# Attention, top-1 mixture of experts and gated MLP on one core: paced scatters of token numbers, five gating groups, and the last four tiles' rows on GpSimd's queue

## The chip, the core and the metric

One core of a Trainium2 chip runs the whole program. The metric is device time of one execution in microseconds (us). Before the change the median of three runs is 1510.78 us (1508.44 to 1511.18). The engines are TensorE (PE; PEld is its weight load), VectorE (DVE), ScalarE (ACT), GpSimd (POOL) and SyncE (SP), which here only issues DMAs.

## The reference, cut to what matters

```python
k_p, v_p = mean over groups of 8 tokens of k, v        # 576 -> 72 keys per head
attn = softmax(q @ k_p.T / sqrt(64)); x = attn @ v_p   # (8, 8, 576, 64)
x = x.transpose(0, 2, 1, 3).reshape(4608, 512)

logits = x @ w_gate; e_idx = argmax(logits)            # 8 experts, one per token
gate_w = softmax(logits)[e_idx]; eom = sigmoid(x @ w_output_gate)
out[token] = gate_w * eom[e_idx] * (relu(x @ w1[e_idx]) @ w2[e_idx])

h = out @ w_in; return (h * sigmoid(h)) @ w_out        # 512 -> 2048 -> 512
```

## The kernel before

The program has three stages: attention with the gating (to about 217 us of the profiled execution), the expert products (to about 700 us), and the gated MLP. All order is written out by hand: an engine runs its instructions in the order in which the Python code emits them, and so does each DMA queue.

**Attention.** The 4608 tokens are 36 tiles of 128 (`NT`). A tile is two steps `u` (four heads each), so the main loop runs `u` from 2 to 74. A step turns the probabilities of one half tile on TensorE (`turn_p`, line 485), copies them on ScalarE (`copy_p`, line 489: this copy occurs once in each step, and the text counts steps by it), takes maxima on VectorE (line 473), exponentials on ScalarE (line 479), multiplies by the values (line 500) and makes the scores of a later step (line 463). At even steps `rows_out` divides a tile's sums on VectorE into `xg` (line 520) and stores the tile's 128 rows of 2 KB to DRAM, `xd` (line 527): tiles 0 to 31 from SP's queue, tiles 32 to 35 from ScalarE's (`ACT_AT = 32`). A table, `plan`, filled by `at(u, f)`, says what else a step starts: loads of q in packets of 128 bytes (line 340), loads of k and v, their sums over 8 tokens on GpSimd (`pool_kv`, lines 358 to 364), zeroing of value tiles (`start_v`, lines 375 and 376). A second list, `item`, holds the transposes of the pooled keys and values (`tr_k` line 394, `tr_v` line 413, `rows_v` line 426), one for each step from its due step on.

**Gating.** Tiles are taken in groups, `GROUPS = (16, 8, 6, 6)`. When the last tile of a group has its gate values, the 20 operations of `gate_ops` (lines 551 to 618) go on the list `bgq`, from which each step takes two to four (`bg`): maximum, winning expert, rank of each token among those of its expert (`rank`, on TensorE, lines 566 and 569), slot number `sli`, and weight, which lands in `idw` beside the token's number. Then `scatter(i)` (lines 580 and 581) writes the 128 pairs (token number, weight) of one tile, 8 bytes each, into `idd`, a table in DRAM sorted by expert, with an indirect DMA of GpSimd's queue whose row numbers are `sli`. Ahead of each stands one memset of a single element, `spacer`. `SCAT` says at which step each scatter is emitted; as GpSimd's stream goes on without waiting for steps, a scatter starts when what stands ahead of it on GpSimd is done and its group's `idw` is there. Those of the last group and those due after the loop come in the next stage's head (`pre[-2]`, `pre[-0.5]`).

**Early item.** After the first 24 tiles (`EARLY = 2` groups) the expert with the most tokens is known: `early_ops` finds it, an indirect DMA fetches 384 of its token numbers (`e_gid`, line 638, at step `EG`), and at step `ET` they are copied and turned to `e_ids`. With these, GpSimd gathers the first item's rows from `xd` (line 1104, `gather_x`), so that the expert stage can start (transposes at line 1126, first product at line 1156) before the last group is gated.

Of the kernel before, what the change touches and what calls it, by code (L numbers as in the profile page):

```python
# [25 lines left out]
POOL = 8  # L26
NK = S // POOL
NT = N // P
GROUPS = (16, 8, 6, 6)
NG = len(GROUPS)  # L30
N9 = NK // 8
SB = B // 2
KPARTS = ((0, 4), (4, 8), (8, 9))
G0 = [sum(GROUPS[:g]) for g in range(NG)]
NBLK = N // P
# [2 lines left out]
KINDS = (3, 2, 1)  # L38
NKD = len(KINDS)
SLOTS = ((NBLK - 3 + E - 1) // 3, 2 * E, E)  # L40
EARLY = 2
REST = N - 3 * P
TB = 384
PREP = 112
# [18 lines left out]
QPB = 5  # L63
QA = 3
PVL = 3
ACT_AT = 32
EG = 63
ET = 70

SCAT = ((11, 3), (5, 3), (6, 2))  # L70
LOADS = (
# [44 lines left out]
def kernel(  # L116
# [14 lines left out]
    nc = tc.nc  # L131
# [55 lines left out]
    spacer = const.tile([1, 1], F32, tag="spacer", name="spacer")  # L187
# [134 lines left out]
    sums, vbt, qz_t, rank_t, bgq, evac, items_q, scq = {}, {}, {}, [], [], [], [], []  # L322
# [59 lines left out]
    def flush():  # L382
        while evac:
            evac.pop(0)()
# [123 lines left out]
    def o4(t):  # L508
        return pv_t[t].rearrange("p a (h c) -> p a h c", c=VW)
# [8 lines left out]
    def rows_out(t):  # L518
        xg = gx.tile([P, DM], F32, tag="xg", name=f"xg{t}")
        nc.vector.tensor_tensor(  # L520
            out=xg.rearrange("p (a h d) -> p a h d", a=2, h=4),
            in0=o4(t)[:, :, :, 0:D],
            in1=r_t[t].to_broadcast([P, 2, 4, D]),
            op=ALU.mult,
        )
        eng = nc.scalar if t >= ACT_AT else nc.sync
        return lambda: eng.dma_start(out=xd[t * P : (t + 1) * P, 0:DM], in_=xg)

    def gates(t):
        g = max(j for j in range(NG) if G0[j] <= t)  # L530
        if t == G0[g]:
            gl_t[g] = (lp if g == NG - 1 else gp).tile([P, GROUPS[g], 16], F32, tag="gl", name=f"gl{g}")
        gh = gp.tile([P, 2, 4, 16], F32, tag="gh", name=f"gh{t}")
# [7 lines left out]
    def gate_ops(g, pool, rank_ps):  # L541
        gl = gl_t.pop(g)
        GT = GROUPS[g]
        sh = [P, GT, E]
# [32 lines left out]

        def scatter(i):
            t = G0[g] + i
            nc.gpsimd.memset(spacer, 0.0)  # L580
            ins = nc.gpsimd.indirect_dma_start(
                out=idd,
                out_offset=bass.IndirectOffsetOnAxis(ap=sli[:, i, :], axis=0),
                in_=idw[:, t, :],
                in_offset=None,
            )
            tc.declare_no_dep(ins.ins, group="scat", reason="every token has a slot of its own")
            tc.add_to_no_dep_group("scat", ins.ins)
# [5 lines left out]
        ops = [  # L594
            red(mx, lg, ALU.max),
            tt(cand, lg, bc(mx), ALU.is_equal),
            tt(cand, cand, bc(wrev.unsqueeze(1)), ALU.mult),
            red(best, cand, ALU.max),
            tt(ohb, cand, bc(best), ALU.is_equal),
            rank,  # L600
            tt(oh, cand, bc(best), ALU.is_equal),
            tt(ex[:, :, 0:E], lg, bc(mx), ALU.subtract),
# [141 lines left out]
    def at(u, f, *a):  # L744
        plan.setdefault(u, []).append((f, a))
# [18 lines left out]
    def bg(n):  # L764
        while n and bgq:
            f = bgq[0]
            if f is None:
                bgq.pop(0)
                return
            bgq.pop(0)()  # L770
            n -= 1
# [6 lines left out]
    UN = 2 * NT  # L778
    for u in range(2, UN + PVL):
        for f, a in plan.get(u, ()):  # L780
            f(*a)
        flush()
        if u < UN:
            turn_p(u)
        if u + 2 < UN:
            maxima(u + 2)
        if u < UN:
            copy_p(u)
        if u + 2 < UN:
            exps(u + 2)  # L790
        if u >= PVL:
            values(u - PVL)
        if u + 3 < UN:
            scores(u + 3)
        if item and item[0][0] <= u and not rank_t:
            _, f, *a = item.pop(0)
            f(*a)
        t, odd = divmod(u - PVL - 2, 2)
        if odd == 0 and 0 <= t < NT:
            inverse(t)  # L800
            at(u + 2, rows_out(t))
        if odd and 0 <= t < NT:
            gates(t)
            if t + 1 in G0:
                g = G0.index(t + 1) - 1
                ops, scat = gate_ops(g, gp if g < NG - 2 else lp, rank_ps)
                bgq.extend(ops)
                for i, f in enumerate(scat):
                    v = u + SCAT[g][0] + 2 * i // SCAT[g][1]
                    if v < UN + PVL:  # L810
                        at(v, f)
                    else:
                        kept_scat.append(f)
                if g + 1 == EARLY:
                    ops, ga, tu, tv = early_ops()
                    bgq.extend(ops)
                    at(EG, ga)
                    at(ET, tu)
                    item.append((ET, tv))
        if u % 2 == 0 and QD <= u // 2 + QA < NT:  # L820
            emit_qT(u // 2 + QA)
        bg(2 if u < 52 else 4 if u < 58 or u >= 64 else 3)
    assert not item, item
    bg(len(bgq) + 1)
    flush()
# [537 lines left out]
    with ExitStack() as cctx:  # L1363
# [184 lines left out]
        for n in range(NFP, NFP * NSB):  # L1548
            k11, k21, k22, k12 = (n, 0, 0), (n, 1, 0), (n, 1, 1), (n, 0, 1)
            u, v, t = ctile("u", f"u{n}"), ctile("v", f"v{n}"), ctile("t", f"t{n}")  # L1550
# [72 lines left out]
```

## Time and profile before

| what | value |
|---|---|
| median of three runs | 1510.78 us |
| the profiled execution's own time | 1503.53 us |
| its span, first to last instruction | 1501.8 us |
| busy: PE, PEld | 1438.1 us (96%), 1274.9 us (85%) |
| busy: DVE, ACT, POOL | 935.1, 652.1, 380.4 us |
| mean granted TensorE clock | 0.976 of full speed |

The profiled execution took 1.7 us more than its span, and 7.25 us less than the median of the runs. TensorE is the engine that sets the pace of the whole program, but a busy TensorE is not one at full speed: its clock is granted at one of two levels, 2.4 GHz (1.00 in the profile) and 1.2 GHz (0.50), and its busy time counts both alike. So the first thing to look for is where its clock is below 1.00, and the second what stood still just before.

### The profile page before, as it was taken

The numbers are of one execution on the slowest core, as the hardware profiler recorded it, in microseconds if no ns is written. First come the engines' busy times: TensorE is split into PE (matmuls) and PEld (weight loads), VectorE is DVE, ScalarE is ACT, GpSimd is POOL, SyncE is SP. The second block draws the span as 40 slices with busy tenths as digits, with TensorE's granted clock in tenths as the row PEclk, the third lists the DMA queues.
The fourth block names the chain that finished last, engine by engine and source line by source line (L and its number), as shares of the span: only waits on it lengthen the run. The fifth ranks groups of instructions, "written<-read, shape, count | busy, mean of one in ns | idle before, by whom it ended". The sixth has DMA issues, their size and how long they took to land.

```text
span 1501.8 us, 21992 instructions
## 1 busy us (share of the span) xinstructions
PE 1438.1 (96%) x7924; PEld 1274.9 (85%) x7924; DVE 935.1 (62%) x1691; ACT 652.1 (43%) x1311; POOL 380.4 (25%) x445
## 2 busy tenths in 40 slices
PE   8998978899999999999999999999999999999996
PEld 6897867789889989898888898888888888898885
DVE  6675556698888778884762645555554555465443
ACT  4765343465665554663332423432343243234222
POOL 1766222345445534431011200030030012001001
PEclk9998688999999999999999999999999999999998
DMA  9999145687788876874989565476457647645441
GB/s 261 274 249 150 36 132 165 218 271 239 265 288 285 298 226 224 296 232 134 309 298 255 212 174 169 161 197 174 156 175 167 183 154 197 178 139 190 160 134 43
DMA packets 259624, 302.87 MB, mean 202 GB/s; under 512 B 157848, under 2 KB 190619, under 8 KB 250674
## 3 DMA queue, kind: packets, MB, share of 16 engines
q1 hardware_dynamic: 247042, 271.06, 61.7%
q0 software_dynamic: 11456, 28.48, 5.2%
q10 hardware_dynamic: 1008, 1.84, 0.4%
q8 instruction: 64, 1.05, 0.3%
q14 instruction: 54, 0.44, 0.1%
HBM read 251.70 MB, written 50.41 MB: 201 GB/s over the span
## 4 chain that ended last, share of the span: by engine, by line
PE 43%; DVE 4%; ACT 3%; issue 1%; SPq 0%; DMA 0%; POOL 0%; another core or an unknown queue 0%; DVEq 0%; ACTq 0%; POOLq 0%
PE o L1437 23%; PE b L1393 9%; PE a L1393 6%; DVE sg L1411 1%; ACT gh L1414 1%; DVE gl L1419 1%; ACT ems L1509 1%; DVE W L1499 1%; SPq L969 0%; DMA yin<-yd 0%; ACT os L1447 0%; ACT b L993 0%; DVE ems L1510 0%; DVE b L994 0%; POOL out_dram L1449 0%
## 5 line engine op out<-in xcount | busy, mean ns | idle before, releaser
L1437 PE MATMUL o<-woh,gh 128*128 128x512 f32 x576 | 229.2, 398 | 2.9 <-ACT gh L1414 2.4
L1437 PE MATMUL o<-woh,gl 128*128 128x512 f32 x576 | 229.5, 398 | 0.0
L1437 PE MATMUL o<-wol,gh 128*128 128x512 f32 x576 | 225.5, 391 | 0.0
L1449 POOL DMA_INDIRECT out_dram<-os,ids x33 | 35.7, 1082 | 623.3 <-ACT os L1447 619.4
L1414 ACT CAST gh<-sg 128x384 fp32r<-128x384 f32 x192 | 98.6, 513 | 148.7 <-DVE sg L1411 145.4
L1419 DVE TENSOR_TENSOR gl<-sg,gh 128x384 fp32r<-128x384 f32 x192 | 107.3, 559 | 75.5 <-ACT gh L1414 64.6
L1437 PEld LDWEIGHTS o<-woh,gl 128*128 128x128 f32 x576 | 107.9, 187 | 29.7 <-DVE gl L1419 3.5
L1437 PEld LDWEIGHTS o<-woh,gh 128*128 128x128 f32 x576 | 108.0, 188 | 22.2 <-ACT gh L1414 6.4
L1437 PEld LDWEIGHTS o<-wol,gh 128*128 128x128 f32 x576 | 108.2, 188 | 18.1
L1393 PE MATMUL a<-b,wA 128*128 128x384 f32 x480 | 97.4, 339 | 2.3 <-issue 1.8
L1393 PE MATMUL b<-t,wS 128*128 128x384 f32 x480 | 97.2, 337 | 0.2
L1407 ACT ACTIVATE sg<-a 128x384 f32<-128x384 f32 x56 | 27.5, 490 | 160.9 <-PE a L1393 160.9
L1393 PEld LDWEIGHTS a<-b,wA 128*128 128x128 f32 x480 | 85.2, 188 | 7.0 <-issue 2.7
L500 PE MATMUL pv<-vb,pT 72*128 72x128 f32 (+1 forms) x640 | 88.8, 293 | 1.4 <-issue 1.0
L1393 PEld LDWEIGHTS b<-t,wS 128*128 128x128 f32 x480 | 85.4, 188 | 5.5 <-DVE u L1402 1.8
L500 PEld LDWEIGHTS pv<-vb,pT 72*128 72x128 f32 (+1 forms) x640 | 80.9, 197 | 4.0 <-issue 3.4
L1402 DVE TENSOR_TENSOR u<-b,t 128x384 f32<-128x384 f32 x40 | 22.3, 557 | 88.6 <-PE b L1393 88.6
L489 ACT COPY pT<-psp 72x512 f32<-72x512 f32 x72 | 41.8, 581 | 63.7 <-PE psp L485 48.7
L1407 ACT ACTIVATE sg<-t 128x384 f32<-128x384 f32 x40 | 21.1, 527 | 110.2 <-DVE t L1402 104.0
L479 ACT ACTIVATE pe<-sc,nm 128x72 f32<-128x72 f32 x288 | 67.7, 319 | 1.9 <-DVE nm L473 1.6
L473 DVE TENSOR_REDUCE nm<-sc 128x4 f32<-128x288 f32 x72 | 32.4, 452 | 46.5 <-PE sc L463 23.6
L1411 DVE TENSOR_TENSOR sg<-a,sg 128x384 f32<-128x384 f32 x56 | 31.1, 555 | 47.3 <-ACT sg L1407 47.3
(3792 smaller groups left out, 3586.7 us busy)
## 6 DMA issues: line engine op xcount, KB each, us to landing
wS<-wis SPq DMA_DIRECT2D x40, 1024.0 KB
wA<-wid SPq DMA_DIRECT2D x40, 768.0 KB
wol<-wold SPq DMA_DIRECT2D x112, 256.0 KB
wQ<-wid SPq DMA_DIRECT2D x16, 1024.0 KB
yin<-yd SPq DMA_DIRECT2D x44, 192.0 KB
xd<-xg SPq DMA_DIRECT2D x32, 256.0 KB
raw_i<-in_moe_w_in_dram SPq DMA_DIRECT2D x16, 512.0 KB
wid<-em SPq DMA_DIRECT2D x8, 1024.0 KB
```

The lines of the kernel that those rows point to most:

```text
L473: nc.vector.tensor_reduce(out=nm_t[u], in_=sc_t[u], op=ALU.max, axis=AX.X, negate=True)
L479: nc.scalar.activation(out=pe[:, h * NK : h * NK + NK], in_=ps[:, h, :], func=AF.Exp, bias=nm[:, h, :])
L489: nc.scalar.copy(out=pT_t[u], in_=ps_t.pop(u))
L500: nc.tensor.matmul(pv_t[t][o : o + n, j % 2, VW * c : VW * c + VW], pT[:, j, o : o + n], vw[b][:, HG * h : HG * h + VW], start=True, stop= ...
L1393: nc.tensor.matmul(ps, w[:, o, i, c, :], x[:, c, :], start=(first and k == 0), stop=(k == 5), skip_group_check=True)
L1402: nc.vector.tensor_tensor(out=o, in0=a, in1=b, op=ALU.add)
L1407: nc.scalar.activation(out=g_t[key][0], in_=h, func=AF.Sigmoid)
L1411: nc.vector.tensor_tensor(out=sg, in0=h, in1=sg, op=ALU.mult)
L1414: nc.scalar.copy(out=gh, in_=sg)
L1419: nc.vector.tensor_tensor(out=gl, in0=sg, in1=gh.bitcast(F32), op=ALU.subtract)
L1437: nc.tensor.matmul(o_t[sb, a][s], x[:, sl_], w, start=(k0 == 0 and k == 0), stop=(k0 == 2 * NFP - 1 and k == 2))
L1449: ins = nc.gpsimd.indirect_dma_start(out=out, out_offset=bass.IndirectOffsetOnAxis(ap=(id_t[b][:, s, 0:1] if b else e_ids[:, s : s + 1]), ...
```

## The change

- The first gating group of 16 tiles becomes two of 8: `GROUPS = (8, 8, 8, 6, 6)`; the early item still comes after 24 tiles (`EARLY = 3`). The first group's operations start at step 26 (`GAT`), and steps 26 to 31 take four operations each.
- `SCAT` gives each of the first groups one scatter per step, the first group's from step 31, the second's from step 46, the third's from step 57.
- Each scatter has six memsets of `spacer` ahead of it (`PACE = 6`) where it had one. Each memset writes the element that the one before wrote, and waits for it.
- The row stores of tiles 32 to 35 move from ScalarE's queue to GpSimd's (`POOL_AT`).
- The early fetch and its turn move from steps 63 and 70 to 66 and 72.

```diff
-GROUPS = (16, 8, 6, 6)
+GROUPS = (8, 8, 8, 6, 6)
-EARLY = 2
+EARLY = 3
+PACE = 6
-ACT_AT = 32
-EG = 63
-ET = 70
-SCAT = ((11, 3), (5, 3), (6, 2))
+POOL_AT = 32
+EG = 66
+ET = 72
+GAT = {0: 26}
+SCAT = ((11, 2), (10, 2), (5, 2), (6, 2))
...
-        eng = nc.scalar if t >= ACT_AT else nc.sync
+        eng = nc.gpsimd if t >= POOL_AT else nc.sync
         return lambda: eng.dma_start(out=xd[t * P : (t + 1) * P, 0:DM], in_=xg)
...
-            nc.gpsimd.memset(spacer, 0.0)
+            for _ in range(PACE):
+                nc.gpsimd.memset(spacer, 0.0)
...
-                bgq.extend(ops)
+                (at(GAT[g], bgq.extend, ops) if g in GAT else bgq.extend(ops))
...
-                    v = u + SCAT[g][0] + 2 * i // SCAT[g][1]
-                    if v < UN + PVL:
-                        at(v, f)
+                    step = u + SCAT[g][0] + 2 * i // SCAT[g][1]
+                    if step < UN + PVL:
+                        at(step, f)
...
-        bg(2 if u < 52 else 4 if u < 58 or u >= 64 else 3)
+        bg(3 if 58 <= u < 64 else 4 if u >= 52 or GAT[0] <= u < GAT[0] + 6 else 2)
```

How GpSimd's stream moves around the sums of the last k and v. Names: `kv0_3` is the last k tile, `kv1_3` the last v tile, `ks` their sums, `vb` value tiles, `sli0` the slots of the first group, `idd` the table. Before:

```order
L376 MEMSET vb5_1187 72x8
L358 TENSOR_TENSOR kv0_3_830<-kv0_3_830 128x5x256
...
L364 TENSOR_TENSOR ks0_3_1460<-kv0_3_830 128x1152
L358 TENSOR_TENSOR kv1_3_1113<-kv1_3_1113 128x5x256
...
L364 TENSOR_TENSOR ks1_3_1465<-kv1_3_1113 128x576
L375 MEMSET vb6_1817 72x47
...
L580 MEMSET spacer_120 1x1
L581 DMA idd_89<-idw_97,sli0_0_1561 37888x2
```

Now (line numbers are two or three higher than before):

```order
L378 MEMSET vb5_1201 72x8
L583 MEMSET spacer_120 1x1 x6
L584 DMA idd_89<-idw_97,sli0_0_1016 37888x2
...
L360 TENSOR_TENSOR kv0_3_831<-kv0_3_831 128x5x256
...
L366 TENSOR_TENSOR ks0_3_1519<-kv0_3_831 128x1152
...
L366 TENSOR_TENSOR ks1_3_1524<-kv1_3_1127 128x576
```

Three scatters of the first group now stand ahead of these sums and five between them and the value tiles; before, all sixteen stood behind them.

How GpSimd's stream moves at the end of the attention. Names: `e_gid` the early fetch, `sli2` (before) and `sli3` (now) the slots of the group of tiles 24 to 29, `xg32` to `xg35` the rows of the last four tiles, `xt` the gathers of the first item, `gid` the later fetch of all token numbers. Before:

```order
L638 DMA e_gid_2162<-idd_89,e_row_2161 3x256
L580 MEMSET spacer_120 1x1
L581 DMA idd_89<-idw_97,sli2_2_2580 37888x2
...
L1104 DMA xt0_0_-1_0_2959<-xd_86,e_ids_149 128x512
L1104 DMA xt1_0_-1_0_2961<-xd_86,e_ids_149 128x512
L1104 DMA xt2_0_-1_0_2963<-xd_86,e_ids_149 128x512
...
L581 DMA idd_89<-idw_97,sli3_3_2956 37888x2
...
L875 DMA gid_2893<-idd_89,rowi_2891 79x256
```

Now:

```order
L641 DMA e_gid_2283<-idd_89,e_row_2282 3x256
L583 MEMSET spacer_120 1x1 x6
L584 DMA idd_89<-idw_97,sli3_3_2733 37888x2
...
L529 DMA xd_86<-xg32_2907 128x512
...
L529 DMA xd_86<-xg34_2991 128x512
L529 DMA xd_86<-xg35_3014 128x512
L1107 DMA xt0_0_-1_0_3138<-xd_86,e_ids_150 128x512
...
L584 DMA idd_89<-idw_97,sli4_4_3135 37888x2
...
L878 DMA gid_3072<-idd_89,rowi_3070 79x256
```

Five scatters stand ahead of the three gathers as before (the sixth of the group behind them), but the four row stores now stand among and behind those five, and the gathers behind `xg35`, the last rows that the attention makes.

The same place on ScalarE before, where `pT` is the copy of a step and `ex_3` the last group's exponential:

```order
L489 COPY pT70_2763<-psp70_2758 72x512
L527 DMA xd_86<-xg32_2753 128x512
L489 COPY pT71_2785<-psp71_2780 72x512
L527 DMA xd_86<-xg33_2795 128x512
L527 DMA xd_86<-xg34_2817 128x512
L527 DMA xd_86<-xg35_2835 128x512
L605 ACTIVATE ex_3_2952<-ex_3_2952 128x6x9
```

The four stores leave this stream, and the exponential follows the last copy directly.

## Rows read from the trace of the kernel before

**Rows 1.** The page: granted TensorE clock in 40 slices of 37.5 us.

```profile
PEclk9998688999999999999999999999999999999998
```

**Rows 2.** Windows: length, busy PE, PEld, DVE, ACT, POOL (instructions), clock, DMA share, GB/s.

```profile
104.00:129.00 25.00, 23.63 (x235) 22.76 (x234) 22.95 (x68) 18.00 (x61) 9.79 (x9) 1.00 1.08 251
129.00:133.00 4.00, 4.00 (x39) 3.79 (x39) 3.12 (x9) 2.91 (x13) 3.09 (x5) 1.00 1.48 152
133.00:136.00 3.00, 3.00 (x32) 2.62 (x30) 0.11 (x1) 2.07 (x6) 2.34 (x6) 1.00 1.22 178
136.00:140.00 4.00, 2.53 (x16) 1.32 (x13) 0.00 (x0) 0.00 (x0) 3.32 (x7) 1.00 1.07 211
140.00:145.00 5.00, 0.50 (x2) 0.20 (x3) 2.48 (x8) 1.23 (x4) 2.47 (x5) 0.57 0.21 32
145.00:165.00 20.00, 20.00 (x98) 17.86 (x99) 7.47 (x21) 6.67 (x25) 5.75 (x12) 0.50 0.08 27
185.00:190.00 5.00, 3.15 (x18) 2.47 (x16) 0.28 (x1) 0.61 (x3) 2.61 (x5) 0.50 0.17 47
215.00:223.00 8.00, 2.29 (x16) 1.94 (x16) 0.59 (x3) 0.58 (x1) 5.04 (x7) 0.76 1.08 246
```

**Rows 3.** Timeline of ScalarE, copies of steps 27, 37, 46, 56, 58, 63, 70, 71.

```profile
84.87 0.58 ACT L489 COPY pT<-psp 72x512 f32<-72x512 f32 x1
...
109.74 0.58 ACT L489 COPY pT<-psp 72x512 f32<-72x512 f32 x1 [0.40 <-PE psp L485]
...
130.51 0.58 ACT L489 COPY pT<-psp 72x512 f32<-72x512 f32 x1
...
175.98 0.58 ACT L489 COPY pT<-psp 72x512 f32<-72x512 f32 x1 [1.17 <-PE psp L485]
...
179.63 0.58 ACT L489 COPY pT<-psp 72x512 f32<-72x512 f32 x1 [0.34 <-PE psp L485]
...
197.10 0.58 ACT L489 COPY pT<-psp 72x512 f32<-72x512 f32 x1 [0.59 <-PE psp L485]
...
211.33 0.58 ACT L489 COPY pT<-psp 72x512 f32<-72x512 f32 x1
...
215.62 0.58 ACT L489 COPY pT<-psp 72x512 f32<-72x512 f32 x1 [3.70 <-PE pv L500]
```

**Rows 4.** Timeline of GpSimd: start, duration, operation, idle before it and its releaser.

```profile
91.59 5.21 POOL L358 TENSOR_TENSOR kv<-kv 128x1280 f32<-128x1280 f32 x2 [4.71 <-DMA kv<-in_k_dram]
96.88 2.62 POOL L362 TENSOR_TENSOR kv<-kv 128x1152 f32<-128x1152 f32 x1
...
130.62 0.09 POOL L580 MEMSET spacer<- 1x1 f32 x1
130.92 0.97 POOL L581 DMA_INDIRECT idd<-idw,sli  x1 [0.20 <-issue]
...
209.90 1.03 POOL L581 DMA_INDIRECT idd<-idw,sli  x1 [17.40 <-DVE idw L618]
...
218.88 0.95 POOL L1104 DMA_INDIRECT xt_-1_0_2963<-xd,e_ids  x1 [0.30 <-issue]
```

**Rows 5.** Timeline of all engines: last keys' transpose, attention's end, later fetch.

```profile
124.85 0.60 PE L394 MATMUL trk<-ident,ks 128*128 128x128 f32 x4
...
211.41 0.35 ACTq L527 DMA_DIRECT2D xd<-xg  x1
...
212.33 0.63 PE L485 MATMUL psp<-ident,pe 128*72 128x128 f32 x4
...
222.71 0.17 DVE L513 TENSOR_SCALAR r<-pv 128x8 f32<-128x8 f32 x1 [7.37 <-remote]
...
227.68 1.08 PE L1126 MATMUL trx_-1_0_3026<-ident,xt_-1_0_2959 128*128 128x128 f32 x4
227.77 0.25 ACT L605 ACTIVATE ex<-ex 128x54 f32<-128x54 f32 x1 [11.58 <-DMA xd<-xg]
...
246.98 2.05 POOL L875 DMA_INDIRECT gid<-idd,rowi  x1 [9.33 <-PE y_-1_0_3123 L1202]
```

## The prediction

> **What bounds the kernel now.** I read the page's clock line first. It shows TensorE at full speed all through, but for the fourth to the seventh slice, 112 to 262 us [rows 1]. So the place is the second half of the attention and the start of the expert stage, and a gain can only come from there. The windows of that stretch come next [rows 2]. From 104 to 129 us TensorE is busy 23.63 of 25 us at clock 1.00. Then the engines stop one after the other: from 133 to 136 us VectorE works 0.11 us, from 136 to 140 us VectorE and ScalarE not at all, and TensorE 2.53 of 4 us; from 140 to 145 us TensorE has 0.50 us. After that it runs at clock 0.50, the 1.2 GHz level, in all of the window from 145 to 165 us. The same happens twice more, shorter: 185 to 190 us (VectorE 0.28, ScalarE 0.61 of 5 us, clock 0.50), and 215 to 223 us (TensorE 2.29 of 8 us).
>
> What is common to the three? GpSimd alone goes on working (3.32 of 4, 2.61 of 5, 5.04 of 8 us), and its timeline shows what it does: scatters back to back, the next one 0.09 us of memset, 0.20 of issue and 0.97 of scatter behind the last, a period of 1.26 us [rows 4]. The DMA engines are loaded at the first and third (shares 1.07 and 1.08), less at the second (0.17) [rows 2]. Spacing alone does not stop the engines: in the window from 145 to 165 us, which takes the rest of the sixteen scatters at a DMA share of 0.08, TensorE is busy all 20 us. So I read the stops as scatters close together on top of other transfers. The profile shows the coincidence, not the link: it names no real releaser for these waits ("remote", as in the 7.37 us wait of VectorE [rows 5]).
>
> What a stop costs is read from ScalarE's copies, one per step [rows 3]. **First stop:** steps 46 to 56 take 175.98 - 130.51 = 45.5 us. Steps 27 to 37, which carry the same side work (a set of values turned and multiplied), take 109.74 - 84.87 = 24.9 us. The stop and the slow clock behind it cost 20.6 us; I count 19, since the gating work in the two stretches is not quite equal. **Second stop:** steps 58 to 63 take 17.5 us; steps 63 to 70 go at (211.33 - 197.10) / 7 = 2.03 us each, so five would take 10.2: 7.3 us lost. **Third stop:** it lies at the attention's end and is costed below with the tail.
>
> **The change part by part.** *Six memsets for one, and one scatter per step.* Five more memsets in a chain. The trace has no chain of memsets; a memset is 0.09 us, and a GpSimd operation that needs the one before starts 0.08 us after its end (91.59 + 5.21 to 96.88) [rows 4]. Low end: five times 0.09, the period is 1.71 us. High end: five times 0.09 + 0.20, the wait ahead of a scatter, 2.71 us. I take 0.17 each, because a chained memset is nearest to that row: 1.26 + 0.85 = 2.11 us. That is about a step (2.03 us), so the density of scatters falls by 40%. GpSimd itself pays 36 times 0.85 = 31 us, which lies in its idle time, except at the tail.
>
> *Five groups.* Of the first sixteen scatters three now start near step 31, by the copies' pace of 2.49 us about 95 us, and push the sums of the last keys back: before 91.59 to about 102 us, now about 101 to 112 us. Their use is the transpose at 124.85 us [rows 5], so this costs nothing; if the first group's `idw` were over 12 us late, the cover would be gone and TensorE would wait. Five more follow the sums of the values, and eight come from step 46 on. So the stretch of the first stop still gets scatters, but about 13 of them 2.11 us apart, where 16 came 1.26 us apart. One more gating group adds 19 VectorE operations at some 0.17 us (the small operation at 222.71 [rows 5]) = 3.2 us, of which VectorE's free time takes most (22.95 busy of 25 us at its worst [rows 2]); and 16 small matmuls on TensorE, at most 0.16 us each by the four of line 485 in 0.63 us [rows 5]. Nothing to 5.8 us; I take 1.
>
> *Stops gone.* If the stops go, -19 - 7.3 = -26.3 us. Bounds: 0, and -27.9 with the full 20.6.
>
> *Stores of four tiles on GpSimd.* On ScalarE the store of tile 32 is issued at 211.41 us, and the copy of step 71 right behind it starts at 215.62 us though its input was there at 212.33 + 0.63 = 212.96 us [rows 3, 5]: 2.7 us that go. The 11.58 us that ScalarE waits ahead of the last group's exponential are not the stores' fault: VectorE stands still until 222.71 us and the exponential at 227.77 us needs its result [rows 5]. On GpSimd the price of a store of 128 rows of 2 KB is not shown; the nearest row is the gather of as many, 0.95 + 0.30 = 1.25 us [rows 4]. For moving plain stores the Trainium skill's page "DMA: Bandwidth & Descriptors", section "Issuing engine by pattern", has a rule that speaks against the change: simple loads and stores belong on the hardware queues, and only indirect ones on GpSimd's. Its first-byte figures (about 1 us against 0.6) would add at most 1.6 us to the sum for four stores, an estimate from that page; no run here shows it yet.
>
> *The tail.* Behind the stores on GpSimd stand the first item's three gathers, then seven scatters and the later fetch `gid`. The chain starts at 209.90 us [rows 4]: five scatters at 2.11 and four stores at 1.25 are 15.6 us, so the first gather is issued at 225.5 and done issuing at 226.5 us; before, the third was issued at 218.88 us. How long a gather takes to land lies between 0 and 8.8 us (218.88 to the first transpose at 227.68 us, in the clogged stretch [rows 4, 5]). I take 2 us, near the low end, as the clog should be gone: first transpose at 228.5 us, against 227.68 us before. With the low ends it comes 3 us earlier, with the high ends about 10 us later. So the third stop gives nothing: VectorE may be 7 us earlier with the last group, but the gathers are late next. I take +1. The last seven scatters end near 229 + 14.8 = 244 us, ahead of the 246.98 us at which `gid` was issued [rows 5].
>
> **Sum.** -26.3 + 1 + 1 = -24.3 us against the profiled execution's 1503.5 us: 1479.2 us. That execution lies 7.25 us under the median. If that gap is longer stops in other executions, it goes with them; if not, it stays. I add half: **1482 us**. A measurement here tells about 0.2% (3 us) from no change.
>
> **The rivals.** *Half gone.* Scatters at 2.11 us still meet row stores and q loads around 130 us, and some engines stop for two or three microseconds, or TensorE's clock still falls once. For it: the stops in rows 2 need only a few scatters. Against: the same spacing in a quiet stretch did no harm. 13 us of 26.3 saved, 2 paid: about 1496 us.
>
> *Not what it says: it is the writes, not their spacing.* If the tiny writes themselves clog the DMA engines whenever other transfers run, all 36 scatters still come, thirteen of them in the same loaded stretch, and the stops only move. For it: the quiet stretch at the same spacing was harmless, so load matters. Nothing saved, 2 us paid: 1513 us, within 0.2%. The same page of the Trainium skill, "DMA: Bandwidth & Descriptors", section "Specifications", says that transfers under 512 bytes make the DMA engine read, modify and write; that would charge by the count of writes, which stays.
>
> *Slower: GpSimd's queue becomes the bound at the attention's end.* The three gathers stand behind five paced scatters and four stores, the last of which needs the attention's last rows. It decides if a scatter's period is near 2.7 us and landing slow: the first transpose comes 10 us later than now, and TensorE idles and starts the expert stage at 1.2 GHz. It gives a slower kernel only where the stops give back less than those 10 us: with nothing saved and little hidden, 1510.8 + 8 = 1519 us.
>
> **How the numbers follow.** Forecast 0.52 (1468 to 1490 us by its bounds), half gone 0.25 (1489 to 1504), writes 0.10 (1508 to 1514), slower 0.13 (above 1514). Faster: 0.52 + 0.25 = 0.77; same 0.10; slower 0.13. The range from 1466 to 1508 us holds the first two and leaves out the others; the forecast's own range is 1468 to 1490.
>
> **What would show it.** Right: no window from 128 to 200 us in which VectorE and ScalarE both do nothing for 3 us; clock 1.00 from 104 to about 190 us; steps 46 to 56 in about 26 us; a scatter period near 2.1 us; and the attention's last copy near 188 us. The first transpose of the expert stage should come some 15 us after that copy, waiting for `xt`. Wrong: clock 0.50 for 20 us or more before the last copy; scatters 2.1 us apart with VectorE idle beside them (the writes); a wait of over 20 us between the last copy and that transpose (the queue); or a new wait of VectorE for `e_gid` at step 72.

## The result, and the profile after

The changed kernel takes 1487.11 us (median of 4 runs, 1484.67 to 1489.32), the kernel before 1510.98 us (4 runs, 1508.44 to 1511.65): ratio 0.9845, 95% interval 0.9825 to 0.9864. Its profiled execution took 1487.75 us, 15.8 us less than that of before.

The page's clock line is now low in one slice, from 186 to 223 us, where four were low, apart from the last slice in both [rows 1]:

```profile
PEclk9999979999999999999999999999999999999998
```

The windows of [rows 2] in the changed kernel (busy time of TensorE, its weight loads, VectorE, ScalarE and GpSimd with the count of instructions, then granted clock, DMA share and GB/s):

```profile
104.00:129.00 25.00, 22.12 (x197) 20.64 (x197) 20.83 (x54) 13.82 (x49) 23.34 (x29) 0.93 1.10 234
...
133.00:136.00 3.00, 3.00 (x29) 3.00 (x27) 2.20 (x9) 2.96 (x10) 1.26 (x12) 1.00 0.77 96
136.00:140.00 4.00, 4.00 (x41) 3.79 (x40) 3.07 (x8) 3.96 (x15) 3.11 (x15) 1.00 0.86 116
140.00:145.00 5.00, 5.00 (x46) 4.44 (x45) 2.37 (x7) 2.96 (x10) 3.99 (x18) 1.00 1.06 256
145.00:165.00 20.00, 19.56 (x188) 18.39 (x187) 16.60 (x57) 12.51 (x45) 5.49 (x26) 1.00 0.25 66
...
185.00:190.00 5.00, 5.00 (x46) 4.96 (x45) 4.37 (x18) 4.18 (x15) 1.59 (x8) 1.00 0.50 163
...
197.00:205.00 8.00, 0.50 (x12) 0.42 (x12) 3.55 (x17) 1.30 (x2) 5.59 (x12) 0.50 1.11 178
205.00:215.00 10.00, 5.22 (x17) 3.85 (x18) 2.08 (x3) 1.76 (x3) 6.39 (x29) 0.50 0.50 140
```

From 133 to 165 us no engine stops any more: VectorE works 3.07 of the 4 us from 136, where it did nothing, and the clock stays at 1.00. The second stop is gone too (185 to 190 us). Two things are worse than I expected: the window from 104 to 129 us, and TensorE's idle time at the end of the attention, 197 to 215 us at the 1.2 GHz level.

ScalarE's copies of steps 27, 46, 56, 58, 63, 70 and 71, which answer to [rows 3] (start, us, operation):

```profile
85.34 0.58 ACT L491 COPY pT<-psp 72x512 f32<-72x512 f32 x1
...
137.03 0.58 ACT L491 COPY pT<-psp 72x512 f32<-72x512 f32 x1
...
161.86 0.58 ACT L491 COPY pT<-psp 72x512 f32<-72x512 f32 x1 [0.40 <-PE psp L487]
...
165.51 0.58 ACT L491 COPY pT<-psp 72x512 f32<-72x512 f32 x1
...
175.17 0.58 ACT L491 COPY pT<-psp 72x512 f32<-72x512 f32 x1 [0.40 <-ACT pe L481]
...
189.40 0.58 ACT L491 COPY pT<-psp 72x512 f32<-72x512 f32 x1
190.75 0.58 ACT L491 COPY pT<-psp 72x512 f32<-72x512 f32 x1 [0.77 <-PE psp L487]
```

Steps 46 to 56 take 24.8 us (45.5 before), steps 58 to 63 9.7 (17.5), steps 70 to 71 1.35 (4.29). But step 46 comes at 137.03 instead of 130.51 us: 6.5 us are lost ahead of the place of the first stop. The last copy is 24.9 us earlier, the end 15.8.

GpSimd's timeline, two of the first group's scatters with the six memsets between them, then the end of the attention (the bracket is the idle time before and what ended it):

```profile
126.59 0.97 POOL L584 DMA_INDIRECT idd<-idw,sli  x1 [0.16 <-issue]
127.56 0.82 POOL L583 MEMSET spacer<- 1x1 f32 x6
128.54 0.97 POOL L584 DMA_INDIRECT idd<-idw,sli  x1 [0.16 <-issue]
...
190.96 0.60 POOL L529 DMA_DIRECT2D xd<-xg  x1
...
198.03 1.15 POOL L529 DMA_DIRECT2D xd<-xg  x2
199.55 1.00 POOL L1107 DMA_INDIRECT xt_-1_0_3138<-xd,e_ids  x1 [0.37 <-DMA idd<-idw,sli]
```

And TensorE's first transpose of the expert stage:

```profile
208.66 1.12 PE L1129 MATMUL trx_-1_0_3210<-ident,xt_-1_0_3138 128*128 128x128 f32 x4 [10.56 <-DMA xt_-1_0_3138<-xd,e_ids]
```

The scatters' period is 1.95 us, a store on GpSimd 0.6 us. The first gather is issued 8.8 us behind the last copy, and the first transpose comes 9.1 us behind that.

The 6.5 us stand beside GpSimd's sums. In the changed kernel the sums of the last keys and values run from 103.72 to 123.69 us, behind three of the first group's scatters, and VectorE's gating of the second group of eight tiles lies on top of them (`cand`, `best`, `ohb` and `oh` are steps in finding each token's winning expert):

```profile
113.43 1.01 DVE L553 TENSOR_TENSOR cand<-gl,mx 128x64 f32<-128x64 f32 x1
115.76 1.53 DVE L553 TENSOR_TENSOR cand<-cand,wrev 128x64 f32<-128x64 f32 x1
117.33 0.22 DVE L556 TENSOR_REDUCE best<-cand 128x8 f32<-128x64 f32 x1
...
120.92 1.37 DVE L553 TENSOR_TENSOR oh<-cand,best 128x64 f32<-128x64 f32 x1
```

```profile
119.65 0.34 PE L568 MATMUL rank<-ohb,tri 128*128 128x8 bf16 x8 [2.88 <-DVE ohb L553]
```

These operations with two inputs take 1.0 to 1.5 us (a fourth, `ohb`, 0.48), the reduction of one input between them 0.22. TensorE waits 2.88 us for the gating, and the granted clock is 0.93 over the window from 104 to 129 us, where it was 1.00 [rows 2]. The first group's gating lies beside the sums before these: its `cand` takes 1.45 us at 85.44 us, and steps 27 to 30 take 10.9 us against 8.0 before.

### The profile page after: what moved, and what is told of

Read it like the earlier page. It is cut to its first block, busy times and chain, and to the rows that moved or that the text cites. A ratio compares the mean times of both kernels' runs of the same rounds, so it can differ in the third digit from the quotient of the medians.

```text
span 1486.0 us, 22189 instructions
## 1 busy us (share of the span) xinstructions
PE 1424.4 (96%) x7924; PEld 1263.4 (85%) x7924; DVE 940.8 (63%) x1709; ACT 652.5 (44%) x1312; POOL 395.2 (27%) x629
## 4 chain that ended last, share of the span: by engine, by line
PE 42%; DVE 5%; ACT 3%; issue 2%; SPq 1%; DMA 0%; another core or an unknown queue 0%; POOL 0%; DVEq 0%; ACTq 0%; POOLq 0%
PE o L1440 22%; PE b L1396 8%; PE a L1396 6%; DVE sg L1414 1%; ACT gh L1417 1%; DVE gl L1422 1%; SPq L972 1%; DVE W L1502 1%; ACT ems L1512 0%; ACT t L996 0%; ACT os L1450 0%; DMA yin<-yd 0%; ACT sg L1410 0%; DVE b L997 0%; ACT b L996 0%
## 5 line engine op out<-in xcount | busy, mean ns | idle before, releaser
L502 PE MATMUL pv<-vb,pT 72*128 72x128 f32 (+1 forms) x640 | 81.6, 279 | 0.0
L502 PEld LDWEIGHTS pv<-vb,pT 72*128 72x128 f32 (+1 forms) x640 | 74.3, 183 | 1.8 <-issue 1.0
```

Source lines behind the costliest of these rows:

```text
L502: nc.tensor.matmul(pv_t[t][o : o + n, j % 2, VW * c : VW * c + VW], pT[:, j, o : o + n], vw[b][:, HG * h : HG * h + VW], start=True, stop= ...
```

## The experiments

Twelve runs in four batches, each batch on a chip of its own. All runs of a batch share its chip, the kernel before among them; ratios are to the kernel before of the same batch. No chip was measured in two batches, so what differs from chip to chip can't be told from anything else that goes with a batch; "chip" stands for both. The first theory was that of the prediction: scatters 1.26 us apart, on top of other transfers, stop the engines, and the memsets alone bring the gain. Its rivals: the split into groups, the later places or the stores bring it; or the writes do the harm, however far apart.

**First batch: what brings the gain.** The kernel before took 1510.24 us (13 runs, 1502.98 to 1516.61).

*One memset in the changed kernel.*

```diff
-PACE = 6
+PACE = 1
```

> The changed kernel with one memset ahead of each scatter instead of six; all else as changed. Theory (the stops come from scatters 1.27 us apart on top of other transfers, and the spacing of 1.95 us removes them): the stops come back where scatters run back to back, VectorE and ScalarE stand still for 3 us or more near 130 to 150 us or near 170 to 185 us, TensorE's clock falls to 0.50 behind it, and steps 46 to 63 cost 10 to 28 us more than the 51.6 us to step 71 less its end; about 1500 to 1512 us. Rival (the split into groups of 8 and one scatter per step do it, not the memsets): within 3 us of the changed kernel's 1487 us, no window with both engines idle.

1504.72 us (10 runs, 1496.98 to 1517.25), ratio 0.9964 (0.9931 to 0.9996). The stops are back. Windows of this kernel:

```profile
145.00:150.00 5.00, 3.99 (x31) 2.97 (x29) 0.48 (x1) 1.77 (x6) 4.19 (x8) 1.00 0.17 53
150.00:155.00 5.00, 3.28 (x18) 2.69 (x16) 2.23 (x7) 2.22 (x7) 1.05 (x2) 0.66 0.07 5
155.00:165.00 10.00, 10.00 (x50) 8.95 (x50) 3.88 (x11) 2.97 (x11) 0.00 (x0) 0.50 0.07 26
```

VectorE works 0.48 of 5 us, and TensorE goes on at 1.2 GHz. Steps 46 to 56 take 37.6 us, steps 58 to 63 17.7. So the five groups, the stores and the places of the scatters don't remove the stops; the memsets do. Without them the rest of the change is worth 5.5 us, with an interval that ends just short of 1. The stop needs no loaded DMA engine either: the share is 0.17 here.

*Six memsets in the kernel before, nothing else.*

```diff
-            nc.gpsimd.memset(spacer, 0.0)
+            for _ in range(6):
+                nc.gpsimd.memset(spacer, 0.0)
```

> The kernel before with six memsets ahead of each scatter of token numbers and nothing else of the change: groups of 16, 8, 6, 6, stores on ScalarE. Theory (spacing alone removes the first two stops, 20.6 and 7.8 us in the traces): steps 46 to 63 near 36 us as in the changed kernel (32 to 36), no added loss at steps 27 to 30, about 1480 to 1488 us. Rival (sixteen scatters in the loaded stretch clog it at any spacing, the split is needed): a stop remains near 135 us with a clock of 0.50 behind it, 1498 us or more.

1484.37 us (4 runs, 1479.24 to 1484.58), ratio 0.9834 (0.9796 to 0.9871); steps 46 to 56 24.8 us, steps 58 to 63 9.7. Within these intervals the memsets alone give all of the gain. The other three parts of the change add nothing to it that these runs can tell. But the memsets are not free here. The spacing makes the early fetch late, VectorE waits 3.71 us for it, and steps 70 to 71 take 5.1 us:

```profile
189.31 0.21 DVE L675 CAST e_gif<-e_gid 3x128 f32<-3x128 int32 x1 [3.71 <-DMA e_gid<-idd,e_row]
```

The changed kernel turns that fetch at step 72 instead of 70 and has no such wait.

*The stores back on ScalarE, in the changed kernel.*

```diff
-        eng = nc.gpsimd if t >= POOL_AT else nc.sync
+        eng = nc.scalar if t >= POOL_AT else nc.sync
```

> The changed kernel with the four last row stores back on ScalarE's queue. Theory (GpSimd's queue delays the first item's gathers, which then land late): the gathers are issued about 3 us earlier, near 196 us, and the first transpose of the expert stage comes 3 to 8 us earlier; against it the copy of step 71 waits 2 to 3 us behind a store: 1480 to 1487 us. Rival (the move is what frees ScalarE at the end and is worth its place): 2 to 4 us slower, 1489 to 1491 us.

1484.81 us (4 runs), ratio 0.9832 (0.9794 to 0.9870): its interval overlaps that of the change, so the time doesn't tell where the stores should stand. The trace shows more. The first gather is issued 6.4 us behind the last copy, where it was 8.8 with the stores on GpSimd. And the copy of step 71, which I expected to wait 2 to 3 us behind a store on ScalarE, waits for its input alone, a miss:

```profile
191.48 0.35 ACTq L529 DMA_DIRECT2D xd<-xg  x1
...
192.76 0.58 ACT L491 COPY pT<-psp 72x512 f32<-72x512 f32 x1 [0.78 <-PE psp L487]
```

It comes 1.36 us behind the copy of step 70, as in the changed kernel (1.35).

*The fourth group's scatters behind the first gathers.*

```diff
-SCAT = ((11, 2), (10, 2), (5, 2), (6, 2))
+SCAT = ((11, 2), (10, 2), (5, 2), (11, 2))
```

> The changed kernel with all six scatters of tiles 24 to 29 behind the first item's gathers on GpSimd's queue, where five stood ahead. Theory (the gathers take 9.1 us from issue to first use because scatters and stores clog the DMA engines, and start late because they queue behind them): first gather issued near 196 us, first transpose near 200 us in place of 208.7, the later fetch of token numbers at most 3 us late: 1478 to 1484 us. Rival (the weights' loads and the row stores clog the DMA engines without scatters): the gathers still take 7 us or more to land, gain under 4 us, or the later fetch is late by as much as was won: 1484 to 1490 us.

1489.72 us (4 runs), ratio 0.9866 (0.9828 to 0.9903): a miss in time, and in the range of the rival. The first transpose came 11.7 us behind the last copy (196.93 to 208.63 us) instead of 17.9. Of these 6.2 us, 1.8 are from an earlier issue of the gather (7.0 us behind the last copy), and 4.4 from a shorter time between its issue and the transpose (4.7 us instead of 9.1): without the scatters ahead of it its rows came sooner. But in that execution steps 27 to 46, which the edit doesn't touch, took 59.2 us, against 51.7 in the changed kernel, and put the last copy 6.2 us later. And behind the first transpose another 7.6 us were lost: twelve scatters now stand between the first gathers and the later fetch `gid`, which is issued at 241.80 us instead of 228.21, and TensorE waits 9.06 us for the numbers that it brings. That is the rival as it was put down: the later fetch is late by as much as was won.

**Second batch: the 6.5 us ahead of step 46, and the dose.** This batch ran on another chip, and there the kernel before took 1480.16 us (31 runs, 1475.17 to 1484.51). No run of it comes near the 1503 us of the first batch's quickest.

*GpSimd's sums ahead of the first scatters, gating at steps 29 and 41.*

```diff
-GAT = {0: 26}
-SCAT = ((11, 2), (10, 2), (5, 2), (6, 2))
+GAT = {0: 29, 1: 41}
+SCAT = ((16, 2), (10, 2), (5, 2), (6, 2))
...
-        bg(3 if 58 <= u < 64 else 4 if u >= 52 or GAT[0] <= u < GAT[0] + 6 else 2)
+        bg(3 if 58 <= u < 64 else 4 if u >= 52 or any(a <= u < a + 6 for a in GAT.values()) else 2)
```

> The changed kernel with group 0 gated from step 29 and group 1 from step 41 (each over six steps at four pieces a step), and group 0's scatters from five steps later, so that GpSimd's sums of the last keys and values run before them. Theory (gating beside GpSimd's sums costs the 6.1 us by which steps 27 to 46 take 51.7 us in the changed kernel against 45.6 before): steps 27 to 46 near 46 to 48 us, VectorE's cand and oh rows at 0.2 us instead of 1.4 to 1.5, about 1482 to 1483 us. Rival (the split into five groups costs by its extra work, wherever it stands): steps 27 to 46 still 50 to 52 us, 1487 us as before.

1479.36 us (10 runs, 1476.97 to 1495.63), ratio 1.0005 (0.9976 to 1.0034). Steps 27 to 46 took 46.1 us, as expected; the time can't be set against 1487 us, which is of another chip (it is repeated below).

*The same, with the fourth group's scatters behind the gathers.* The edit is the one before and `(11, 2)` for the last `(6, 2)`.

> The kernel with the sums first, and the fourth group's scatters behind the first gathers. Theory (the two costs are separate and add): steps 27 to 46 near 47 us, the first gather about 5 us behind the last copy instead of 9, first expert transpose 12 us behind the last copy, about 1478 us. Rival (the tail's gain is eaten by TensorE's half-clock stretch behind the attention, whose length does not depend on it): no faster than the kernel with the sums first alone.

1484.41 us (10 runs), ratio 1.0038 (1.0018 to 1.0059): slower than without, as the rival had it. The first transpose again came as expected (11.8 us behind the last copy, 17.9 without), though the first gather is issued 7.0 us behind that copy and not 5. Part of the loss is at steps 27 to 46, 49.5 us against 46.1. Here the first group's gating met the sums of the last keys. From the timeline of GpSimd and VectorE:

```profile
90.99 5.21 POOL L360 TENSOR_TENSOR kv<-kv 128x1280 f32<-128x1280 f32 x2 [3.95 <-DMA kv<-in_k_dram]
...
91.88 2.09 DVE L553 TENSOR_TENSOR cand<-gl,mx 128x64 f32<-128x64 f32 x1
94.01 2.28 DVE L553 TENSOR_TENSOR cand<-cand,wrev 128x64 f32<-128x64 f32 x1
```

Operations on 64 elements a partition took over 2 us, and TensorE idled until its clock fell:

```profile
95.00:100.00 5.00, 2.21 (x32) 1.83 (x31) 4.93 (x12) 0.96 (x4) 4.84 (x3) 0.82 1.07 167
100.00:105.00 5.00, 5.00 (x28) 4.76 (x25) 3.52 (x11) 2.11 (x7) 2.13 (x1) 0.50 1.29 230
```

Where the gating meets the sums depends on when the keys land and when the steps come (sums from 90.99 us and `cand` from 91.88 us here, 91.59 and 90.77 in the kernel without the last edit), so a gating that is put beside them is a matter of luck.

The larger part of the loss is behind the first transpose: from there to the end this execution takes 9.4 us more than the one without the edit. The later fetch `gid` follows the last of the scatters by 9 to 10 us in both, and here the scatters end 13.3 us later. Without the edit, then with it (`rkf` is the copy of the fetched token numbers):

```profile
221.62 2.05 POOL L878 DMA_INDIRECT gid<-idd,rowi  x1 [9.29 <-PE y_-1_0_3337 L1205]
```

```profile
236.01 1.94 POOL L878 DMA_INDIRECT gid<-idd,rowi  x1 [10.40 <-DMA r_-1_5_3472<-in_moe_w_dram]
...
245.00 0.40 PE L1034 MATMUL psi<-ident,rkf 79*128 79x79 f32 x1 [10.24 <-DVE rkf L1032]
```

TensorE waits 10.24 us for that fetch; without the edit it doesn't wait there.

*Three memsets for six, in the changed kernel.*

```diff
-PACE = 6
+PACE = 3
```

> The changed kernel with three memsets for six: scatter period about 1.26 + 2 x 0.14 = 1.54 us. If the stop sets in with a threshold between 1.26 and 1.95 us that lies above 1.54, steps 46 to 56 take 37 us as with one memset and the time is near 1505; if below, 25 us and 1487. If the stop grows in proportion to the scatters' density, steps 46 to 56 take about 30 us and the time is near 1494.

1483.97 us (10 runs), ratio 1.0029 (1.0010 to 1.0047), steps 46 to 56 24.8 us at a period of 1.51 us. It tells nothing of the dose, since on this chip the kernel before, with one memset, needs no cure.

*The kernel before with six memsets, its third group's scatters behind the gathers.*

```diff
+            for _ in range(6):
...
-SCAT = ((11, 3), (5, 3), (6, 2))
+SCAT = ((11, 3), (5, 3), (11, 2))
```

> The kernel before with six memsets for one, and the scatters of its third group behind the first gathers; four groups and ScalarE's stores as before. Theory (spacing gives the whole gain, the split costs, the gathers stand behind scatters that can wait): steps 46 to 56 25 us, steps 27 to 46 48 us, first gather 5 us behind the last copy instead of 8, 1480 to 1482 us, under both kernels. Rival (the tail gains nothing): 1484 us, as with six memsets alone.

1481.08 us (10 runs), ratio 1.0011 (0.9995 to 1.0026): level with the kernel before, not under it as I expected. The first gather is issued 0.6 us ahead of the last copy, not 5 us behind it. Where there are no stops, the memsets and the gathers' earlier place together don't slow the kernel by anything that can be told; the memsets alone were not run there.

**Third batch: is it the chip?** Two theories were left: on some chips scatters 1.26 us apart stop nothing; or the second chip is quicker as a whole. The batch came to a third chip, whose runs of before are like the second's: 1480.05 us (25 runs, 1475.29 to 1484.00).

> The kernel before, unchanged, with a profile. In the first batch of runs its median was 1510.24 us, in the second, on another chip, 1480.16. Theory (the stop is a property of chip and spacing together: on the second chip scatters 1.26 us apart stop nothing): on the first chip steps 46 to 56 take 45 us and the time is 1510; on the second steps 46 to 56 take 25 us, steps 58 to 63 9.7 us, no window with VectorE and ScalarE idle, clock 1.00 to the last copy, 1480. Rival (the stops are there on the second chip too, and something else is 30 us quicker): steps 46 to 56 take 37 to 45 us at 1480 us.

1481.25 us (10 runs), ratio 1.0002 (0.9987 to 1.0017). The stops are gone without any edit, as the first theory has it. Windows of the kernel before on this chip, which answer to [rows 2]:

```profile
133.00:136.00 3.00, 3.00 (x29) 2.99 (x28) 2.24 (x6) 2.96 (x12) 2.21 (x4) 1.00 1.34 190
136.00:140.00 4.00, 4.00 (x38) 3.43 (x38) 2.32 (x8) 2.87 (x9) 3.20 (x7) 1.00 1.38 271
140.00:145.00 5.00, 5.00 (x49) 4.59 (x48) 2.39 (x7) 2.86 (x12) 4.20 (x8) 1.00 0.41 90
145.00:165.00 20.00, 19.57 (x188) 18.62 (x187) 17.61 (x62) 13.16 (x47) 10.03 (x19) 1.00 0.17 55
```

And GpSimd's scatters in them:

```profile
135.01 0.97 POOL L581 DMA_INDIRECT idd<-idw,sli  x1 [0.21 <-issue]
...
136.28 0.96 POOL L581 DMA_INDIRECT idd<-idw,sli  x1 [0.23 <-issue]
```

The same program, the same period of 1.27 us, a DMA share of 1.38 where the stop of [rows 2] stood at 1.07, and every engine goes on. Steps 46 to 56 take 24.8 us, steps 58 to 63 9.7. One sign failed: the clock is not 1.00 to the last copy but 0.93 from 104 to 129 us, and steps 27 to 46 take 48.2 us where the first trace of this kernel had 45.6. In this kernel too the gating can meet the sums (`kv` sums from 111.21 us):

```profile
111.82 2.43 DVE L551 TENSOR_TENSOR cand<-cand,wrev 128x128 f32<-128x128 f32 x1
```

> The changed kernel, unchanged, with a profile, on the same chip as the run before it. Theory (it gives back the stops where there are any, and costs 4 to 7 us beside that): 1487 us on either chip; on a chip without stops that is slower than before by 4 to 7 us (0.3 to 0.5%), of it most in steps 27 to 46, on a chip with stops faster by 24. Rival (the whole chip is quicker, stop or not): the same ratio of 0.985 to before on any chip.

1486.77 us (10 runs, 1483.97 to 1488.38), ratio 1.0044 (1.0031 to 1.0057): on this chip the change makes the kernel slower, by 6.7 us. Of the profiled executions' 6.3 us (spans 1486.6 and 1480.3), 1.9 are there at the last copy, the tail up to the first transpose adds 5.2, and 0.8 come back by the end. I expected most of it in steps 27 to 46, a miss: these take 49.2 us against 48.2. GpSimd's queue shows where it is. The kernel before, then the changed one (ScalarE's last copy, GpSimd's first gather, TensorE's first transpose):

```profile
188.69 0.58 ACT L489 COPY pT<-psp 72x512 f32<-72x512 f32 x1 [1.14 <-DVE r L516]
...
191.96 0.99 POOL L1104 DMA_INDIRECT xt_-1_0_2959<-xd,e_ids  x1 [0.30 <-DVE gh L534]
...
203.93 1.11 PE L1126 MATMUL trx_-1_0_3026<-ident,xt_-1_0_2959 128*128 128x128 f32 x4 [8.37 <-DMA xt_-1_0_2959<-xd,e_ids]
```

```profile
190.59 0.58 ACT L491 COPY pT<-psp 72x512 f32<-72x512 f32 x1 [0.78 <-PE psp L487]
...
199.92 1.57 POOL L1107 DMA_INDIRECT xt_-1_0_3138<-xd,e_ids  x1 [0.92 <-DMA idd<-idw,sli]
...
210.98 1.12 PE L1129 MATMUL trx_-1_0_3210<-ident,xt_-1_0_3138 128*128 128x128 f32 x4 [13.09 <-DMA xt_-1_0_3138<-xd,e_ids]
```

The first gather is issued 9.3 us behind the last copy instead of 3.3: paced scatters and stores stand ahead of it. From the gather to the transpose it is 11.1 us instead of 12.0.

*The sums first, again.* The kernel of the second batch, beside the changed one on one chip.

> The kernel with GpSimd's sums of the last keys and values ahead of the first group's scatters and gating, again, beside the changed kernel on the same chip. Theory (gating and scatters beside those sums cost about 5 us): 4 to 6 us under the changed kernel's time of the same call, steps 27 to 46 near 46 us. Rival: within 2 us of it.

1482.79 us (10 runs, 1478.75 to 1491.93), ratio 1.0027 (1.0005 to 1.0048), 4.0 us under the changed kernel, at the edge of what was expected, but the intervals of the two ratios overlap. In the traces, one execution of each, steps 27 to 46 took 45.9 us against 49.2.

**Last: gating clear of the sums.** If sums and gating don't go together, the kernel before has such a place too: steps 37 to 40 took 10.5 us in the second batch's version of it, with its `cand` rows beside the sums of the values:

```profile
111.24 1.12 DVE L551 TENSOR_TENSOR cand<-gl,mx 128x128 f32<-128x128 f32 x1
...
113.68 1.04 DVE L551 TENSOR_TENSOR cand<-cand,wrev 128x128 f32<-128x128 f32 x1
```

The edit, to that version (four groups, six memsets, third group's scatters behind the gathers):

```diff
-                bgq.extend(ops)
+                (at(41, bgq.extend, ops) if g == 0 else bgq.extend(ops))
...
-        bg(2 if u < 52 else 4 if u < 58 or u >= 64 else 3)
+        bg(4 if 41 <= u < 46 else 2 if u < 52 else 4 if u < 58 or u >= 64 else 3)
```

> Four groups, six memsets and the third group's scatters behind the first gathers, and now the first group's gating put from steps 36 to 45 (beside GpSimd's sums of the last values, 109 to 119 us) to steps 41 to 45, where GpSimd has no sum. Theory (VectorE's two-input operations beside those sums cost the 5 us by which steps 37 to 40 take 10.5 us instead of 5.5): steps 37 to 40 in 5.5 to 6.5 us, no cand row over 0.4 us, no 3.4-us fall of the clock near 119 us, steps 46 to 56 still 25 us, time 1476 to 1478 us; against the kernel before 0.997 on a chip where that one needs 1480, 0.978 on one where it needs 1510. Rival (the five us are the work itself, or come back as a wait later): steps 37 to 46 together still 23 us or more, 1481 us.

1476.85 us (6 runs, 1473.24 to 1481.02) on a fourth chip, where the kernel before took 1510.74 us (11 runs, 1505.14 to 1520.14): ratio 0.9778 (0.9743 to 0.9814), below that of the change. Steps 37 to 40 took 5.5 us, steps 37 to 46 together 20.2 us against 23.8, so nothing came back as a later wait. And the same two operations, behind the sums' end (GpSimd's last sum, then VectorE):

```profile
117.38 1.40 POOL L364 TENSOR_TENSOR ks<-kv 128x576 f32<-128x576 f32 x1
...
119.43 0.29 DVE L551 TENSOR_TENSOR cand<-gl,mx 128x128 f32<-128x128 f32 x1
119.76 0.29 DVE L551 TENSOR_TENSOR cand<-cand,wrev 128x128 f32<-128x128 f32 x1
```

0.29 us each, not 1.12 and 1.04. By its ratio this version beats the change on a chip with stops, though the two were not run on one chip. On a chip without stops it was not run.

## Why the prediction was right, and where it was not

The forecast was 1482 us, the result is 1487.11, inside the range, and faster as forecast. On the chip of the third batch the same sum would have been wrong, and wrong in its sign (1486.77 us against 1480.05).

*The stops.* Right: -20.6 us for the first, where I took -19 from bounds of 0 to -20.6, and -7.8 for the second, where I took -7.3. With both gone whole, "half gone" is out. That spacing removes them on a chip that has them was shown from both sides: with one memset they return, with six alone they go. What failed is "scatters close together on top of other transfers". Close scatters are needed where stops come; but the kernel before on the third chip has them, under more transfers, without a stop, and the kernel with one memset stops at a DMA share of 0.17. Whether there is a stop is decided by something that goes with the chip or the batch, which the profile doesn't show. The kernel before was read on one chip, and a wait that the profile gives no releaser for ("remote", "issue") was taken for a property of the program.

*The writes.* This rival is out. The writes stay 36, and the stops go with the spacing. The Trainium skill's page "DMA: Bandwidth & Descriptors", section "Specifications", has transfers under 512 bytes done by read-modify-write, which I took as a charge by their count; the runs show no harm that follows the count.

*The memsets.* Period 1.95 us against 2.11: 0.82 us for six in a chain, 0.14 each, where I took 0.17. On GpSimd they cost nothing while it is idle, as argued. But they delay what waits for the last scatter: in the four-group kernel VectorE waits 3.71 us for the early fetch with them. In the changed kernel, with the later turn, the wait that I gave as a sign of being wrong didn't come.

*"Five groups", +1 us.* Mis-sized: +6.5 us at step 46 in the two traces that I compared, and with it went the sign "clock 1.00 from 104 to about 190 us". Part of the 6.5 us looks like good luck of the kernel before in that one execution: its steps 27 to 46 took 45.6 us there, but 48.2 in its second trace and with six memsets alone. In the third batch's pair step 46 comes 2.3 us later, of which 1.0 us lies in steps 27 to 46. I bounded the gating by the count of its operations, 0 to 5.8 us, those of VectorE at 0.17 us each (19 by my count, the code has 18), and priced the sums that were pushed back as hidden, because their use came later. I didn't ask what the sums do to VectorE while they run, though the gating was moved on top of them. The runs with the sums first, and the last version, show the price of that meeting. The Trainium skill's page "SBUF — State Buffer", section "Who interferes with whom", has the rule that I passed over: a VectorE instruction with two inputs in SBUF contends with a GpSimd instruction that reads SBUF, and a reduction doesn't. The traces agree: operations of two inputs took 1.0 to 2.4 us in the rows shown beside the sums and 0.29 clear of them, while the reduction beside them took 0.22.

*The tail, +1 us.* Measured: 2.9 us from step 70 to the first transpose (1.35 instead of 4.29 for the last step, 17.9 instead of 12.1 us behind it), and 3.2 us more by the end. The last step fell by 2.9 us, but not by the move that I gave 2.7 for. With the stores back on ScalarE it takes 1.36 us too, and in the kernel before on the third chip, with its stores on ScalarE, 1.72. So a store ahead of the copy doesn't hold it up by itself; what held it up in the first trace is gone where the stops are gone. The stores were cheaper than I took (0.6 against 1.25 us), but they delay the gathers: with the stores on ScalarE the first gather is issued 6.4 us behind the last copy, not 8.8. The gather's landing was not 2 us but 8.1, counted as I counted from the end of its issue (9.1 from the start), near the high end of its bounds (8.8). I held the clog to be the stops', but the DMA share is still 1.11 from 197 to 205 us, and with the five scatters behind the gathers the 9.1 us became 4.7.

*The sum.* Stops -28.4, groups +6.5, tail +2.9 and +3.2: -15.8 us against -24.3. (By its own terms my sum gives 1482.8 us, not 1482.) That the result came so near is in part luck, as another choice failed the other way: I kept half of the 7.25 us between the profiled execution and the median, and the changed kernel has none of it (1487.75 in the profile, 1487.11 in the median). That the gap was longer stops in other executions, which went too, fits their mean clock (0.969 at 1516.61 us, 0.977 at 1502.98 in the first batch), but it isn't shown: only one of them was traced.

*The rival "slower".* Its place, GpSimd's queue between the last copy and the first gather, is the one that decides where there are no stops to give back. I priced it at 1519 - 1510.8 = 8 us; the third chip shows 6.7 us between the medians, and in the traces 5.2 us in the tail. For moving the stores, the Trainium skill's page "DMA: Bandwidth & Descriptors", section "Issuing engine by pattern", has plain stores on the hardware queues. On ScalarE's queue the time was 1484.81 us against 1487.11, not measured together, and the intervals of their ratios overlap: the 1.6 us that I worked out from the page can't be told.

**What stays open.** What it is about a chip that lets close scatters stop the engines, whether it is the chip or something else that goes with a batch, and what the stopped engines wait for. In the packet records of the two profiles of the kernel before, the 41857 packets of 2048 bytes take 0.102 us on average on the chip with stops and 0.101 on the one without, so it is not that transfers are slower throughout; such a mean doesn't tell of the few in a stop. How many memsets are enough was not told either, as the run with three came to a chip without stops. The 3.2 us between the first transpose and the end were not tried; in the third batch's pair the changed kernel is 0.8 us quicker there.

## What to carry to other kernels

A stop whose rows name no releaser is first to be looked for on a second chip, before a kernel is bent around it; a cure that costs little where it isn't needed is the one to keep (here the kernel with six memsets and the gathers ahead was level with the kernel before on a chip without stops). A side task that is moved must be set against what the other engines do at its new place: the gating of a few operations cost most where it met GpSimd's sums. And what stands ahead of the first item's gather on its queue at a stage's end is counted one by one, and so is what stands ahead of the fetch behind it: five scatters that were put behind the gathers brought the first transpose 6 us nearer to the last copy, and TensorE then waited 9 to 10 us at the later fetch.

## What the runs showed of the hardware

- One program takes 1480 us on two chips and 1510 on two others (25 to 31 runs each on the first, 11 and 13 on the second), with no overlap: 1484.5 at most against 1503.0 at least. On the slower kind, scatters 1.26 us apart stop the engines (VectorE's waits of 7.88 and 5.57 us in the kernel before, 7.22 with one memset in the changed one), and 1.95 us apart they don't.
- The price of the meeting of VectorE's two-input operations with GpSimd's sums is set by chance: the sums start when the keys land, and the same placing of the gating gave `cand` rows of 2.09 and 2.28 us in one kernel (steps 27 to 46 in 49.5 us) and left steps 27 to 46 at 46.1 us in another of the same batch.
- From the issue of the first item's first gather to the use of its rows it took 6.4 to 12.0 us with five scatters ahead of it on GpSimd's queue (nine traces in which TensorE waits for these rows), and 4.7 and 4.8 us with them behind it (two).
